# New queue orders for VectorE, ScalarE and GpSimd, and 54 waits of GpSimd for VectorE

## The chip, the cores and the metric

One Trainium2 chip; the kernel runs on one of its NeuronCores. The metric is the device time of one launch in microseconds. In the profile the engines are PE (TensorE, matmuls), PEld (its weight loads), DVE (VectorE), ACT (ScalarE), POOL (GpSimd) and SP (SyncE, which here issues the DMAs). L312 and the like are lines of the kernel before.

## The reference

A block with attention and a gated feed-forward part, both fed by the same normalised rows (sequence S = 2048, width D = 512, F = 1792, 32 heads of 16, a sliding window of 256), all float32:

```python
def _A_ref(x, wqkv, wo):                     # H = 32, Dh = 16, W = 256
    qkv = (x @ wqkv).reshape(B, S, 3, H, Dh).transpose(2, 0, 3, 1, 4)
    q, k, v = qkv[0], qkv[1], qkv[2]
    scores = jnp.einsum("bhqd,bhkd->bhqk", q, k) * (Dh ** -0.5)
    mask = (idx[:, None] - idx[None, :] >= 0) & (idx[:, None] - idx[None, :] < W)
    p = _softmax(jnp.where(mask[None, None], scores, -1e9), axis=-1)
    o = jnp.einsum("bhqk,bhkd->bhqd", p, v)
    return o.transpose(0, 2, 1, 3).reshape(B, S, D) @ wo

def _B_ref(x, w1, w3, w2):
    h = _silu(x @ w1) * (x @ w3)
    return h @ w2

xn = _layernorm(A_x, axis=-1)
return A_x + _A_ref(xn, A_wqkv, A_wo) * _silu(_B_ref(xn, B_w1, B_w3, B_w2))
```

## The kernel before, in words

**Arithmetic.** Every float32 operand of a large product is scaled and cut into two float16 parts, a high one and the rest (the low one), and a product is three matmul terms (high by high, low by high, high by low) that add up in a PSUM bank. So each weight tile of 128 by 512 costs, beside its load, a high part (ScalarE) and a subtraction for the low part, on VectorE or on GpSimd. `split` (L310 to L312) writes the high part on ScalarE (L311) and the low part in one VectorE operation (L312). `split_pool` (L319 to L323) scales the tile and copies the high part on ScalarE (L320, L321), and subtracts in four pieces on GpSimd (L323).

**Tiling.** The sequence is cut into four tiles of 512 rows. For each, the kernel projects q, k and v (L539, L572, L587 to L590), takes the maxima of the scores in a first pass (L637, L650), computes scores, their exponentials and the product with v in a second (L720 on TensorE, L726 the mask on VectorE, L728 the exponential on ScalarE, L746 on TensorE), and normalises the heads' outputs (L317 and L814 on GpSimd). Between these, in the same tile, stand the large products of the feed-forward part: gate and up (`gate_up`, L1004; its tanh on ScalarE is L1018, the two VectorE operations behind it are L1021 and L1025, its high part L1034 on ScalarE and its low part L317 on GpSimd), and down (L1224 in the first two tiles). In the last two tiles the down product is done by a scheme of seven products on combined halves (`fold_weights`, `fold_first`, `fold_second`; L1144), whose sums and cuts are GpSimd's work: L963 to L966 add the weight halves, L972 copies a high part on ScalarE, L975 copies one on GpSimd, L976 subtracts the low part. The sum of a row block with the attention's output is `total` (L1267 a tanh on ScalarE, L1268 on VectorE, L1273 on TensorE, L1276 and L1278 on VectorE); the last block is done in two halves by columns (`total_by_columns`, L1300 to L1310), each with a store of its own.

**Buffers.** 54 numbered slots of SBUF hold raw weights, cut parts and activations in turn; a program name such as slot53_832 is slot 53 with the number of the instruction that took it. Weights are squared and summed first (L230 and L894 on ScalarE) for a scale per tile, and only then cut.

**Order.** TensorE runs in the order in which the program is written. For VectorE, ScalarE, GpSimd and SyncE a table of numbers in `QUEUES` (L1608) gives the order: number k is the k-th instruction that the program makes for that engine, and `queue` chains each instruction to the one ahead of it, so that the engine issues them in that order. Semaphores between engines come from the data alone: a read after a write, or a buffer that is taken again. SyncE's table sets in which order the loads and stores are issued, each when its buffer's last user is done.

The place that the prediction dwells on is this pair in `total`:

```python
nc.scalar.activation(y, acc, AF.Tanh, scale=0.5)                                            # L1267
nc.vector.scalar_tensor_tensor(y, y, 1.0, acc, op0=ALU.add, op1=ALU.mult)                   # L1268
```

Of the kernel before, what the change touches and what calls it, by code (L numbers as in the profile page):

```python
# [17 lines left out]
ENGINE = mybir.EngineType  # L18
# [62 lines left out]
def tile_block(ctx: ExitStack, tc: tile.TileContext, x, wqkv, wo, w1, w3, w2, out):  # L81
# [1518 lines left out]
    for n, b in enumerate((1, 3, 0)):  # L1600
# [139 lines left out]
```

## Time and profile before

| | |
|---|---|
| median of 3 runs | 809.68 us (807.79 to 810.52) |
| the profiled execution | 809.6 us, of which the span of its instructions is 807.8 us |
| TensorE busy | 791.1 us (98%), 9181 matmuls |
| VectorE busy | 622.9 us (77%) |
| ScalarE busy | 394.8 us (49%) |
| GpSimd busy | 382.2 us (47%) |
| mean granted TensorE clock | 0.995 |

The profile is of one execution. A row of the timeline reads: start and length in us, engine, line and operation, what it writes and reads, how many instructions the row joins, and in brackets the idle time of the engine ahead of it and what ended that. Instructions of one engine overlap a little: the next one starts some 0.1 us before the one ahead ends, so the distance from start to start is what an instruction costs its queue. The view of waits lists for TensorE, per pair of line and releaser, the time waited in all, how often, and the longest. The view of windows gives busy time per engine and stretch, the granted clock, the share of time in which the DMA engines were busy, and GB/s.

### The profile page before, as it was taken

Reading aid. Unit: us, or ns where it says so; the run is one execution under the profiler, and the core shown is the slowest. Engines: PE = TensorE matmul, PEld = TensorE weight load, DVE = VectorE, ACT = ScalarE, POOL = GpSimd, SP = SyncE. Lnnn points to the kernel's source line nnn. Section 1 sums busy time; section 2 is a strip of 40 time slices with the busy share of each in tenths; the row PEclk is TensorE's granted clock in tenths of the full one; section 3 lists DMA queues with packets and bytes.
Section 4 is the critical chain, followed back from the end, with each engine's and each line's share of the span. In section 5 each row is a group of like instructions: output and inputs, shape, how many; then the busy total and the mean of one; then the engine's idle time right before and its main releaser. Section 6 shows DMA issues by size and latency. Waiting matters only on the chain.

```text
span 807.8 us, 23938 instructions
## 1 busy us (share of the span) xinstructions
PE 791.1 (98%) x9181; PEld 404.2 (50%) x9181; DVE 622.9 (77%) x2005; ACT 394.8 (49%) x592; POOL 382.2 (47%) x746
## 2 busy tenths in 40 slices
PE   8989999999997999999999999999999999999998
PEld 4434454444543444444444454456544654466465
DVE  8778989877897678777878887766677888775438
ACT  8779976734364355334534433444444344444411
POOL 2263857732428375265622356530246277550670
PEclk9999999999998999999999999999999999999999
DMA  9768674737563375757465634656462553335431
GB/s 282 220 187 270 218 228 128 250 111 225 161 209 128 103 260 139 237 159 261 132 218 165 185 94 142 165 152 184 121 182 75 161 145 110 111 88 160 127 94 58
DMA packets 109858, 134.18 MB, mean 166 GB/s; under 512 B 18928, under 2 KB 64944, under 8 KB 109744
## 3 DMA queue, kind: packets, MB, share of 16 engines
q1 hardware_dynamic: 109456, 132.13, 54.2%
q8 instruction: 72, 1.18, 0.6%
q10 hardware_dynamic: 288, 0.52, 0.2%
q14 instruction: 42, 0.34, 0.1%
HBM read 91.23 MB, written 36.57 MB: 158 GB/s over the span
## 4 chain that ended last, share of the span: by engine, by line
PE 74%; DVE 8%; DMA 7%; SPq 3%; POOL 3%; ACT 3%; issue 2%; DVEq 0%; ACTq 0%; POOLq 0%
PE m L1004 28%; PE m L1144 8%; PE po L746 8%; PE m L572 7%; PE m L1224 6%; PE s L720 5%; PE m L1273 5%; PE m L539 4%; PE s L637 2%; DMA slot<-in_B_w_dram 2%; DMA dWQ<-slot 2%; POOL slot L323 1%; PE po L637 1%; DVE s L726 1%; DVE junk L650 1%
## 5 line engine op out<-in xcount | busy, mean ns | idle before, releaser
L1004 PE MATMUL m<-XH,slot 128*128 128x512 f16 x896 | 269.0, 382 | 0.1
L728 ACT ACTIVATE pt<-s,es 128x1024 f32<-128x1024 f32 x152 | 167.0, 1113 | 145.2 <-DVE s L726 135.4
L1004 PEld LDWEIGHTS <-slot 128*128 128x128 f16 x1344 | 125.5, 98 | 155.7 <-issue 15.0
L1004 PE MATMUL m<-XL,slot 128*128 128x512 f16 x448 | 170.5, 381 | 0.0
L726 DVE TENSOR_TENSOR s<-s,MK 128x256 f32<-128x256 f32 (+2 forms) x280 | 120.3, 437 | 60.7 <-PE s L720 51.5
L650 DVE CUSTOM_DVE_ANT_0 junk<-s,MW 128x320 bf16<-128x320 f32 x276 | 121.7, 484 | 15.8 <-PE s L637 15.2
L317 POOL TENSOR_TENSOR slot<-slot,slot 128x256 f16<-128x256 f32 (+1 forms) x86 | 58.2, 695 | 90.2 <-ACT slot L1034 41.5
L323 POOL TENSOR_TENSOR slot<-slot,slot 128x128 f16<-128x128 f32 x168 | 66.6, 434 | 50.5 <-ACT slot L321 49.5
L1224 PE MATMUL m<-slot,slot 128*128 128x512 f16 x336 | 78.5, 380 | 0.1
L650 DVE CUSTOM_DVE_ANT_0 junk<-po,MW 128x320 bf16<-128x320 f32 x172 | 77.5, 484 | 0.0
L746 PE MATMUL po<-pt,V 64*32 64x320 f32 (+4 forms) x2880 | 77.2, 342 | 0.0
L572 PE MATMUL m<-XH,slot 128*128 128x512 f16 x240 | 70.8, 380 | 2.1 <-DVE slot L1021 2.1
L1018 ACT ACTIVATE slot<-m,sgs 128x512 f32<-128x512 f32 x56 | 38.3, 685 | 65.6 <-PE m L1004 63.6
L1144 PE MATMUL m<-slot,slot 128*128 128x256 f16 x588 | 68.3, 273 | 0.0
L1059 POOL TENSOR_TENSOR slot<-slot,slot 128x256 f16<-128x256 f32 x98 | 65.0, 672 | 1.5
L720 PE MATMUL s<-qa,KA 50*64 50x320 f16 (+3 forms) x1472 | 58.6, 261 | 6.3 <-ACT pt L728 6.3
L1021 DVE SCALAR_TENSOR_TENSOR slot<-slot,m 128x512 f32<-128x512 f32 x56 | 38.3, 684 | 31.1 <-ACT slot L1018 30.9
L1144 PEld LDWEIGHTS <-slot 128*128 128x128 f16 x588 | 56.2, 98 | 11.1 <-issue 2.7
L746 PEld LDWEIGHTS po<-pt,V 64*32 64x32 f32 x2880 | 50.3, 106 | 22.4 <-issue 0.8
L720 PEld LDWEIGHTS <-KA 50*64 50x64 f16 x1472 | 30.6, 106 | 58.0 <-issue 45.6
L572 PEld LDWEIGHTS <-slot 128*128 128x128 f16 x392 | 36.6, 98 | 44.1 <-issue 3.3
L317 POOL TENSOR_TENSOR on<-on,rb 128x256 f32<-128x256 f32 x32 | 23.3, 745 | 67.6 <-DMA rb<-de 64.4
(194 smaller groups left out, 1148.0 us busy)
## 6 DMA issues: line engine op xcount, KB each, us to landing
slot<-dW SPq DMA_DIRECT2D x98, 256.0 KB
slot<-in_B_w_dram SPq DMA_DIRECT2D x56, 256.0 KB
slot<-dFold SPq DMA_DIRECT2D x48, 256.0 KB
dW<-slot SPq DMA_DIRECT2D x42, 256.0 KB
slot<-in_A_x_dram SPq DMA_DIRECT2D x30, 256.0 KB
KA<-dK SPq DMA_DIRECT2D x24, 288.0 KB
slot<-dWQ SPq DMA_DIRECT2D x24, 256.0 KB
qa<-dQ SPq DMA_DIRECT2D x30, 192.0 KB
```

Source lines behind the costliest of these rows:

```text
L317: op(out[:, c], a[:, c], b[:, c])
L323: nc.gpsimd.tensor_sub(lo[:, c:c + P], raw[:, c:c + P], hi[:, c:c + P])
L572: nc.tensor.matmul(cell["pp"][:, cols[n]], w[:, (a * NC + c) * P:(a * NC + c + 1) * P], b[:, c, cols[n]], start=n == 0 and (c, i) == parts ...
L650: nc.vector.tensor_tensor_reduce(out=junk[:, :n], in0=s[:, r, :n], in1=mask, scale=1.0, scalar=NEG, op0=ALU.add, op1=ALU.max, accum_out=M[ ...
L720: nc.tensor.matmul(s[64 * h:64 * h + 64, r, o:o + 64 * n], ka[rows, 2 * p + a, 64 * (m + 4):64 * (m + 5)], qa[rows, 2 * p + a, 64 * (m + k ...
L726: nc.vector.tensor_add(v, v, MK[:, kind, of:of + n, :].unsqueeze(1).to_broadcast([P, 2 * len(which), n, 64]))
L728: nc.scalar.activation(pt, s, AF.Exp, scale=es)
L746: nc.tensor.matmul(cell["po"][32 * i:32 * i + 32, h, 64 * (m + k):64 * (m + k + n)], V[64 * h:64 * h + 64, (4 * t + m // 2) % VB, hd * VW: ...
L1004: nc.tensor.matmul(cell[k], w[:, (a * NC + c) * P:(a * NC + c + 1) * P], b[:, c, :], start=c == 0 and i == 0, stop=c == NC - 1 and i == 2)
L1059: nc.gpsimd.tensor_sub(lo, view, hi)
L1144: nc.tensor.matmul(cell["ps"][:, c], made[:, f:f + P], wj[:, g:g + 256], start=j == j0 and c == 0 and n == 0, stop=j == j1 - 1 and n == 2, ...
L1224: nc.tensor.matmul(ps, hh[:, a * TW + b * P:a * TW + (b + 1) * P], w[:, c * D:(c + 1) * D], start=f == f0 and i == 0, stop=f == f1 - 1 and ...
```

## The change

No instruction is added, taken out or given other operands. The order tables of VectorE, ScalarE and GpSimd are replaced; TensorE's and SyncE's orders stay as they are. Beside that, `give_way` adds 54 waits across engines, read from a list `TURNS`: in the pair 675-285, GpSimd's instruction 285 waits on a semaphore until VectorE's instruction 675 is done. Instruction numbers are the same as in `QUEUES`; the counting of them is moved into `numbered`. On VectorE's side of the pairs stand five L1268 (675, 705, 1328, 1366 and 1422), and small operations on maxima, scales, means and variances (L242, L277, L281, L283, L420, L424, L425, L452, L667, L668, L853, L854, L898, L918); on GpSimd's side mostly the subtractions and cuts L317, L323, L975, L976, L1058 and L1059.

```diff
 QUEUES = {
     ENGINE.DVE: (
...
-        "52-54 51 55-56 63 57 64 61 66 58 60 65 62 67 59 43 36 49 68 74-77 69 78-79 70 80-81 71 90 72-73 82-84 86-87 85 "
+        "52-54 51 55-56 63-64 57 61 66 60 58 65 62 67 43 36 49 59 68 74-77 69 78-79 70 80-81 71 90 72-73 82-84 86-87 85 "
...
     ENGINE.Activation: (
...
     ENGINE.Pool: (
...
+TURNS = (
+    "203-86 204-86 205-87 195-87 206-92 214-93 251-128 252-129 253-130 287-131 216-117 264-132 217-118 265-121 "
+    "259-134 311-162 312-135 313-140 314-149 315-150 343-171 344-159 362-154 350-204 366-190 431-191 423-210 "
+    "432-214 433-222 519-259 572-270 573-271 675-285 612-310 645-326 646-337 705-361 683-341 721-365 722-366 "
+    "758-392 759-402 795-397 796-399 924-460 1085-533 1223-587 1224-582 1328-622 1299-630 1300-633 1366-628 "
+    "1422-657 1374-676 "
+)
+
+
+def give_way(tc):
+
+
+    made = {e: numbered(tc, e) for e in (ENGINE.DVE, ENGINE.Pool)}
+    for pair in TURNS.split():
+        first, second = map(int, pair.split("-"))
+        tc.add_manual_dep(made[ENGINE.Pool][second], made[ENGINE.DVE][first].name,
+                          mybir.DependencyInfo(mybir.DependencyClass.Sync, mybir.DependencyReason.DATA), reason="turn")
+
+
+def numbered(tc, engine):
+
+
+    return [i for i in tc.nc.cur_bb.bb.instructions if i.engine == engine and i.opcode != "RegisterMove"
+            and not i.opcode.startswith("Tile")]
...
         for engine, order in QUEUES.items():
             queue(tc, engine, order)
+        give_way(tc)
```

**ScalarE's queue, about 45 us into the span** (the first gate products of the first tile). slot53_832 is the tanh of a gate product; the L894 and the L230 are squares of weights just loaded; slot1_907 and slot3_973 are high parts of projections. Before:

```order
L230 ACTIVATE sqa_824,ssq_805<-slot36_699 128x512
L1034 CAST slot46_788<-slot45_734 128x512
L230 ACTIVATE sqa_841,ssq_805<-slot38_703 128x512
L1018 ACTIVATE slot53_832<-m0_809,sgs_155 128x512
L320 ACTIVATE slot18_209<-slot18_209,pi_756 128x512
L894 ACTIVATE sqa_843,ssq2_736<-slot42_711 128x512
L321 CAST slot52_817<-slot18_209 128x512
L230 ACTIVATE sqa_882,ssq_805<-slot37_700 128x512
L587 ACTIVATE slot1_907<-m1_885 128x512
L230 ACTIVATE sqa_899,ssq_805<-slot39_704 128x512
L320 ACTIVATE slot19_210<-slot19_210,pi_756 128x512
L321 CAST slot5_834<-slot19_210 128x512
```

Now:

```order
L1018 ACTIVATE slot53_832<-m0_809,sgs_155 128x512
L230 ACTIVATE sqa_824,ssq_805<-slot36_699 128x512
L320 ACTIVATE slot18_209<-slot18_209,pi_756 128x512
L230 ACTIVATE sqa_841,ssq_805<-slot38_703 128x512
L321 CAST slot52_817<-slot18_209 128x512
L587 ACTIVATE slot1_907<-m1_885 128x512
L894 ACTIVATE sqa_843,ssq2_736<-slot42_711 128x512
L320 ACTIVATE slot19_210<-slot19_210,pi_756 128x512
L230 ACTIVATE sqa_882,ssq_805<-slot37_700 128x512
L321 CAST slot5_834<-slot19_210 128x512
L230 ACTIVATE sqa_899,ssq_805<-slot39_704 128x512
L587 ACTIVATE slot3_973<-m0_912 128x512
```

The tanh L1018 of slot53_832 stood behind two L230 and the L1034 of slot46_788, and stands now ahead of them, directly behind two L894. That L1034 has gone 15 places back, out of this piece. The L587 of slot3_973 ends the piece now; before it stood two places below the piece, behind one more L320 (that of slot20, which now follows it).

**GpSimd's queue, about 239 to 251 us into the span** (the sums and cuts of the folded down weights). The L323 are low parts of weights cut on ScalarE; L975 and L976 cut a folded weight; the two L976 of slot48_4683 are the last readers of slot27_3790, and the L1267 of slot27_5415 on ScalarE, which takes that buffer over, waits for them. Before:

```order
L975 CAST slot24_4642<-slot31_4360 128x256 x2
L976 TENSOR_TENSOR slot24_4642<-slot31_4360,slot24_4642 128x256
L323 TENSOR_TENSOR slot28_4260<-slot51_3582,slot28_4260 128x128 x4
L323 TENSOR_TENSOR slot42_4259<-slot46_3581,slot42_4259 128x128 x4
L323 TENSOR_TENSOR slot30_4262<-slot47_3584,slot30_4262 128x128 x4
L323 TENSOR_TENSOR slot29_4261<-slot14_3583,slot29_4261 128x128
L317 TENSOR_TENSOR slot2_4338<-slot21_4249,slot2_4338 128x256 x2
L323 TENSOR_TENSOR slot29_4261<-slot14_3583,slot29_4261 128x128 x3
L976 TENSOR_TENSOR slot48_4683<-slot27_3790,slot48_4683 128x256 x2
L963 TENSOR_TENSOR slot5_4518<-slot33_4174 128x256
L965 TENSOR_TENSOR slot34_4519<-slot35_4175,slot33_4174 128x256
L964 TENSOR_TENSOR slot5_4518<-slot35_4175,slot5_4518 128x256
```

Now:

```order
L976 TENSOR_TENSOR slot22_4586<-slot45_4361,slot22_4586 128x256
L323 TENSOR_TENSOR slot28_4260<-slot51_3582,slot28_4260 128x128 x4
L323 TENSOR_TENSOR slot42_4259<-slot46_3581,slot42_4259 128x128 x4
L323 TENSOR_TENSOR slot30_4262<-slot47_3584,slot30_4262 128x128 x4
L323 TENSOR_TENSOR slot29_4261<-slot14_3583,slot29_4261 128x128 x2
L317 TENSOR_TENSOR slot2_4338<-slot21_4249,slot2_4338 128x256 x2
L323 TENSOR_TENSOR slot29_4261<-slot14_3583,slot29_4261 128x128 x2
L976 TENSOR_TENSOR slot48_4683<-slot27_3790,slot48_4683 128x256 x2
L963 TENSOR_TENSOR slot5_4518<-slot33_4174 128x256
L965 TENSOR_TENSOR slot34_4519<-slot35_4175,slot33_4174 128x256
L964 TENSOR_TENSOR slot5_4518<-slot35_4175,slot5_4518 128x256
L317 TENSOR_TENSOR slot15_4484<-slot23_4422,slot15_4484 128x256 x2
```

One L976 of slot22_4586 and the two L975 and one L976 of slot24_4642 no longer stand ahead of the L323; they come behind the last row shown. The L317 of slot15_4484, instruction 285, has come forward past one L975 and one L966, and its first half now waits for instruction 675 of VectorE, the L1268 of slot27_5415.

**VectorE's queue at the end of the program** (the last row blocks of the last tile). slot5_13731 is the last block, done in two halves by columns (L1309, L1310). Before:

```order
L1278 TENSOR_TENSOR slot31_13673<-slot31_13673,slot4_13439 128x512
L1278 TENSOR_TENSOR slot19_13694<-slot19_13694,slot38_13441 128x512
L1276 SCALAR_TENSOR_TENSOR slot24_13713<-m0_13712,us_4326,slot24_13713 128x512
L1301 SCALAR_TENSOR_TENSOR slot5_13731<-slot5_13731,slot46_13654 128x512
L1278 TENSOR_TENSOR slot24_13713<-slot24_13713,slot47_13670 128x512
L1309 SCALAR_TENSOR_TENSOR slot5_13731<-m1_13734,us_4326,slot5_13731 128x256
L1310 TENSOR_TENSOR slot5_13731<-slot5_13731,slot43_13691 128x256
L1309 SCALAR_TENSOR_TENSOR slot5_13731<-m0_13750,us_4326,slot5_13731 128x256
L1310 TENSOR_TENSOR slot5_13731<-slot5_13731,slot43_13691 128x256
```

Now:

```order
L1278 TENSOR_TENSOR slot31_13673<-slot31_13673,slot4_13439 128x512
L1276 SCALAR_TENSOR_TENSOR slot24_13713<-m0_13712,us_4326,slot24_13713 128x512
L1301 SCALAR_TENSOR_TENSOR slot5_13731<-slot5_13731,slot46_13654 128x512
L1309 SCALAR_TENSOR_TENSOR slot5_13731<-m1_13734,us_4326,slot5_13731 128x256
L1278 TENSOR_TENSOR slot19_13694<-slot19_13694,slot38_13441 128x512
L1278 TENSOR_TENSOR slot24_13713<-slot24_13713,slot47_13670 128x512
L1309 SCALAR_TENSOR_TENSOR slot5_13731<-m0_13750,us_4326,slot5_13731 128x256
L1310 TENSOR_TENSOR slot5_13731<-slot5_13731,slot43_13691 128x256 x2
```

The first L1309 has moved ahead of the L1278 of slot19 and slot24, and both L1310 stand behind the second L1309.

More of the change, by code (lines that the diff above doesn't have):

```diff
@@ L1702 @@
 }
+TURNS = (
[5 rows of a table added]
+)
[8 more added lines that the diff above has]
+            and not i.opcode.startswith("Tile")]
 def queue(tc, engine, order):
-    made = [i for i in tc.nc.cur_bb.bb.instructions if i.engine == engine and i.opcode != "RegisterMove" and not i.opcode.startswith("Tile")]
+    made = numbered(tc, engine)
     spans = [tuple(map(int, s.split("-"))) for s in order.split()]
     line = [made[k] for s in spans for k in range(s[0], s[-1] + 1)]
-    assert len(line) == len(made), (engine, len(made), len(line), [(i.name, i.opcode) for i in made[:12]], [(i.name, i.opcode) for i in made[-5:]])
+    assert len(line) == len(made)
     for before, after in zip(line, line[1:]):
```

127 rows, old and new, of the table QUEUES are left out of this document.

## The prediction

> **What bounds the kernel now.** First the page's table of busy times:
>
> ```profile
> PE 791.1 (98%) x9181; PEld 404.2 (50%) x9181; DVE 622.9 (77%) x2005; ACT 394.8 (49%) x592; POOL 382.2 (47%) x746
> ```
>
> TensorE is busy for 791.1 of 807.8 us. No instruction goes or comes, so no busy time changes except where a queue was blocked: what an order can win is TensorE's idle time and lost clock. Next, its waits (in all, times, longest):
>
> ```profile
> PE s L720 <- ACT pt L728: 6.3, 3, 5.3
> PE m L572 <- DVE slot L1021: 2.1, 1, 2.1
> PE s L539 <- DVE p2qk L283: 0.7, 1, 0.7
> PE s L637 <- DMA qa<-dQ: 0.2, 1, 0.2
> ```
>
> Third, where they lie, by windows (PE, PEld, DVE, ACT, POOL busy, granted clock, DMA share, GB/s):
>
> ```profile
> 44.00:56.00 12.00, 9.95 (x76) 4.32 (x74) 7.15 (x36) 10.78 (x25) 5.64 (x14) 1.00 0.30 92
> 250.00:256.00 6.00, 1.85 (x9) 0.75 (x8) 5.97 (x4) 2.13 (x4) 4.57 (x8) 1.00 0.12 44
> 256.00:264.00 8.00, 6.68 (x42) 2.86 (x42) 5.85 (x21) 4.33 (x5) 5.13 (x9) 0.57 0.40 131
> 264.00:780.00 516.00, 515.95 (x6438) 266.26 (x6437) 384.21 (x1181) 214.91 (x277) 243.83 (x416) 1.00 0.52 152
> ```
>
> From 264 to 780 us TensorE has no gap: the new orders can win nothing there and can only lose. All that is to be had lies ahead of 264 us, most of it at one place, which also halves the clock (0.57 in the window behind it).
>
> **The stall at 251.9 us.** The timeline there, TensorE first, then ScalarE, VectorE and GpSimd:
>
> ```profile
> 249.09 0.61 PE L1004 MATMUL m<-XH,slot 128*128 128x512 f16 x2
> 251.04 0.59 PE L1004 MATMUL m<-XH,slot 128*128 128x512 f16 x2
> 251.47 0.38 PE L1004 MATMUL m<-XL,slot 128*128 128x512 f16 x1
> 257.18 1.32 PE L720 MATMUL s<-qa,KA 50*64 50x320 f16 x24 [5.33 <-ACT pt L728]
> 258.87 1.01 PE L1004 MATMUL m<-XH,slot 128*128 128x512 f16 x2
> 262.67 0.89 PE L1004 MATMUL m<-XH,slot 128*128 128x512 f16 x2
> ```
>
> ```profile
> 249.28 0.63 ACT L1267 ACTIVATE slot<-slot 128x512 f32<-128x512 f32 x1 [0.86 <-POOL slot L976]
> 256.02 1.11 ACT L728 ACTIVATE pt<-s,es 128x1024 f32<-128x1024 f32 x1 [3.88 <-DVE s L726]
> ```
>
> ```profile
> 249.94 5.17 DVE L1268 SCALAR_TENSOR_TENSOR slot<-slot,slot 128x512 f32<-128x512 f32 x1 [2.56 <-ACT slot L1267]
> 255.03 0.89 DVE L726 TENSOR_TENSOR s<-s,MK 128x256 f32<-128x256 f32 x2
> ```
>
> ```profile
> 237.23 0.74 POOL L975 CAST slot<-slot 128x256 f16<-128x256 f32 x2 [8.05 <-DMA dW<-slot]
> 237.93 1.30 POOL L976 TENSOR_TENSOR slot<-slot,slot 128x256 f16<-128x256 f32 x2
> 240.51 5.06 POOL L323 TENSOR_TENSOR slot<-slot,slot 128x128 f16<-128x128 f32 x13
> 247.94 1.30 POOL L976 TENSOR_TENSOR slot<-slot,slot 128x256 f16<-128x256 f32 x2
> 250.58 0.74 POOL L964 TENSOR_TENSOR slot<-slot,slot 128x256 f32<-128x256 f32 x1
> 252.29 1.30 POOL L317 TENSOR_TENSOR slot<-slot,slot 128x256 f16<-128x256 f32 x2
> 253.89 0.68 POOL L976 TENSOR_TENSOR slot<-slot,slot 128x256 f16<-128x256 f32 x1
> ```
>
> The L1268 lasts 5.17 us, though at the end of the program, with GpSimd quiet, a like one takes 0.69 (the L1278 quoted under the tail, same shape, two SBUF inputs). It ends at 255.11; GpSimd ran without a break from 237.23 to 254.57. So it was let in only when GpSimd stopped, and then took its 0.5 to 0.7. Behind it stand in VectorE's queue the mask L726, then ScalarE's L728, then TensorE's L720.
>
> Two edits meet here. First, one L976, two L975 and one L976 move from ahead of the L323 to behind: 238.58 to 240.51, that is 1.95 us from start to start with the L976's 0.65. The two L976 that release L1267 then end at 249.24 − 1.95 = 247.29, L1267 runs to 247.96, and L1268 is issued at 248.0. Second, GpSimd's L317 (252.29) now waits for it. Ahead of that wait still stand the L964 and its two neighbours, which end at 251.32 − 1.95 = 249.37. Then GpSimd is quiet, and L1268 ends at 249.37 + 0.54 = 249.9, against 255.11: **5.2 us** for L726, L728 and L720. L728 would end at 257.13 − 5.2 = 251.93, TensorE has work to 251.85: the stall closes to a tenth. Queued behind the waiting L317 are its second half, L966, two L975 and further L976, some 0.6 us late against their new place and earlier than in the old one; the moved cuts of slot22 and slot24 come behind those, near where the old run ended, and no row of TensorE waits for a L976. Bounds: 5.33 if the port were free at once; 3.1 if the 1.95 us are not gained but the wait works (L1268 ends at 251.32 + 0.65 = 252.0).
>
> **The clock.** Nine matmuls L1004 took 1.95 us from 249.09 to 251.04 and, after the stall, 3.80 from 258.87 to 262.67: 1.85 us lost, and a little in the 28 matmuls from 257.18; I take **2.1**. The other long idle time, 2.06 us at 49.83, left the clock at 1.00 (first window). So an idle time between 2.06 and 5.33 us is where the loss starts, and a closed stall has none. The Trainium skill, "TensorE: Matmul & The Clock Gate", Part 1, says that the clock halves after an idle window of about 3.4 us and comes back after as much work; the trace agrees at both places. Estimated by it, a rest of stall under 3.4 us would keep the full clock.
>
> **The stall at 47.8 us.**
>
> ```profile
> 46.63 0.63 ACT L230 ACTIVATE sqa<-slot 128x512 bf16<-128x512 f32 x1
> 47.26 0.60 ACT L1034 CAST slot<-slot 128x512 f16<-128x512 f32 x1
> 48.39 0.67 ACT L1018 ACTIVATE slot<-m,sgs 128x512 f32<-128x512 f32 x1
> 49.09 0.69 DVE L1021 SCALAR_TENSOR_TENSOR slot<-slot,m 128x512 f32<-128x512 f32 x1 [3.41 <-ACT slot L1018]
> 49.83 0.59 PE L572 MATMUL m<-XH,slot 128*128 128x512 f16 x2 [2.06 <-DVE slot L1021]
> 54.30 0.57 ACT L587 ACTIVATE slot<-m 128x512 f16<-128x512 f32 x1
> ```
>
> L1018 takes the place of the L230 at 46.63, so L1021 and L572 come 48.39 − 46.63 = 1.76 us earlier (ScalarE shows no idle time ahead of L1018, so its product was ready; how long, no row says). But ScalarE is busy for 10.78 of 12 us here: what is queued behind L1018, the two L230, the cuts and the L587 of 54.30, comes as late as the work ahead of it takes. Of the work ahead of that L587 only the L1034 and one L320 have gone behind it: 0.60 and, like it, 0.6 to 0.7, less 0.1 of overlap each, so it starts near 53.1, 1.2 earlier. Its bank is what the next gate product needs: TensorE gets back about **1.15** of the 1.76, and waits some 0.6 there. Bounds 0.5 (the L1034 alone) and 1.76.
>
> **The two smaller L720.**
>
> ```profile
> 92.97 0.42 PE L720 MATMUL s<-qa,KA 50*64 50x320 f16 x10 [0.45 <-ACT pt L728]
> 159.52 0.42 PE L720 MATMUL s<-qa,KA 50*64 50x320 f16 x10 [0.52 <-ACT pt L728]
> ```
>
> ScalarE's new order puts cuts (L320, L321) behind these L728, and VectorE's puts small operations on scales behind the masks ahead of them, each some 0.6 us, more than either wait: both go, **0.97**; at worst nothing. The waits of L539 and L637 at the start I leave as they are: some small operations pass ahead of VectorE's L312 there, and behind them TensorE waits for the load qa all the same, which covers some tenths; without that cover they would cost about 0.5.
>
> **The tail.**
>
> ```profile
> 802.49 0.69 DVE L1278 TENSOR_TENSOR slot<-slot,slot 128x512 f32<-128x512 f32 x1
> 803.10 0.48 DVE L1309 SCALAR_TENSOR_TENSOR slot<-m,us,slot 128x256 f32<-128x256 f32 x1
> 803.95 0.48 DVE L1309 SCALAR_TENSOR_TENSOR slot<-m,us,slot 128x256 f32<-128x256 f32 x1
> 804.46 0.42 DVE L1310 TENSOR_TENSOR slot<-slot,slot 128x256 f32<-128x256 f32 x1
> ```
>
> The first L1309 now starts where a L1278 did, at 802.49; two L1278 at 0.61 from start to start, the second L1309 and two L1310 follow: 802.49 + 0.51 + 1.22 + 0.51 + 0.34 + 0.42 = 805.5 instead of 804.88, so 0.6 later. The last two stores then leave 0.3 us apart instead of 0.8: **+0.7**, between 0 and 0.9.
>
> **Sum**, against the profiled execution's 809.6 us (1.8 outside the span; the median shown, 809.68, is the same): 809.6 − 5.2 − 2.1 − 1.15 − 0.97 + 0.7 = 800.9, so **801 us**. All bounds at their best give 809.6 − 5.33 − 2.1 − 1.76 − 0.97 = 799.4, and with the 0.9 us of waits at the start 798.5.
>
> **Rivals.** *The stall shrinks, but does not close* (0.17). GpSimd's run begins when a store of folded weights lands (237.23, idle 8.05 before): if that does not move up with the 2 us that TensorE gains earlier, or the 1.95 us are lost, L1268 ends at 252.0, TensorE idles 2.2, and the time is 803; with both, idle 4.3 and the clock lost again, 807. For it: that wait for DMA. Against: that store's data come from the same chain, which moves with TensorE.
>
> *The gain is given back by the next lock* (0.08). Only 54 pairs are named; another L1268 or L726 that meets a run of GpSimd costs again 5.2 + 2.1: 808.2. For it: the orders are all new. Against: over 516 us from 264 TensorE showed no wait in spite of 243.83 us of GpSimd work.
>
> *Slower: the turns hold GpSimd's cuts back* (0.07). 29 of the 54 turns lie between 83 and 160 us, where L1224 reads weights that GpSimd's L323 has just cut, and several of them now stand behind VectorE operations that themselves wait for TensorE. The tightest I find:
>
> ```profile
> 129.24 1.11 ACT L728 ACTIVATE pt<-s,es 128x1024 f32<-128x1024 f32 x1 [0.91 <-DVE s L726]
> 132.44 2.33 PE L1224 MATMUL m<-slot,slot 128*128 128x512 f16 x10
> ```
>
> The L321 that a cut of four L323 needs now stands behind this L728: 130.35, plus 0.6, plus four at 0.39 (5.06 / 13), so 132.5; L1224 reads it some four matmuls into its ten, near 133.3. That leaves under 1 us, and one turn more or less. If each of the 29 cost TensorE 0.4 us, 11.6 would be added to 800.9: 812.5; slower than before from 0.3 each (8.7 / 29). Against: no L323 is among TensorE's waits, and GpSimd is 47% busy.
>
> *The port is let go between two GpSimd instructions* (0.04). Then L1268, issued at 248.0, would end near 249.3 whatever the wait: 800.4. The 5.17 us speak against it, with GpSimd instructions starting at 250.58, 252.29 and 253.89 inside it. The Trainium skill, "SBUF — State Buffer", section "SBUF: two separate sides", states it so: the lock is held for the whole instruction, and the loser waits; here the trace has it wait for a whole run.
>
> **Numbers.** The forecast, with its own range of 799 to 803, has 0.64. The 8-in-10 range is 798 to 806: from all bounds at their best to most of the first rival. About 0.3%, 2.4 us, can be told from no change. Faster: 0.64 + 0.04 + 0.14 + 0.03 of the second = 0.85; same: 0.03 + 0.05 = 0.08; slower: 0.07.
>
> **What would show it.** L1268 near 248 us should last about 2 us instead of 5.17 and L317 on GpSimd start behind it; TensorE's wait for L728 should fall from 6.3 to under 1; the clock should stay at 1.00 in all windows; the wait of L572 for L1021 should be 0.3 or less, with one of about 0.6 a little later. I am wrong if a wait for GpSimd's L323 stands in TensorE's list, or a gap shows after 264 us.

## The result

| | before | changed |
|---|---|---|
| median | 808.80 us (807.79 to 810.52, 4 runs) | 798.58 us (798.28 to 798.97, 4 runs) |
| the profiled execution | 809.6 us, span 807.8 | 798.36 us, span 796.5 |
| mean granted clock | 0.995 | 0.999 |

The ratio is 0.9872, with a 95% interval of 0.9851 to 0.9892: 10.2 us faster, where 801 us were forecast and a range of 798 to 806. The page's busy times after:

```profile
PE 788.6 (99%) x9181; PEld 403.3 (51%) x9181; DVE 616.6 (77%) x2005; ACT 396.1 (50%) x592; POOL 381.3 (48%) x746
```

TensorE's busy time is 2.5 us less with the same 9181 matmuls (the stretch at half clock is gone), VectorE's 6.3 less with the same 2005 instructions. Most of that is time held: the operations that last over 0.2 us longer than the shortest of their line and size are too long by 15.3 us together in the old trace, and by 9.6 in the new one. TensorE's waits after, and its windows:

```profile
PE s L539 <- DVE wvl L312: 1.4, 2, 1.0
PE m L1495 <- DVE onesb L183: 1.0, 1, 1.0
PE m L468 <- DVE slot L452: 0.5, 1, 0.5
PE s L265 <- DVE sb L242: 0.2, 1, 0.2
```

```profile
44.00:56.00 12.00, 12.00 (x95) 5.17 (x93) 8.59 (x41) 11.21 (x26) 4.96 (x14) 1.00 0.47 146
250.00:256.00 6.00, 6.00 (x129) 3.06 (x127) 5.03 (x18) 2.74 (x3) 6.00 (x13) 1.00 0.65 201
256.00:770.00 514.00, 514.00 (x6342) 266.04 (x6340) 381.23 (x1173) 215.41 (x278) 245.24 (x419) 1.00 0.53 153
```

The waits for L728 (6.3 us in all before) and L1021 (2.1) are out of the list; what is left stands in the first 27 us. The window of the big stall, 1.85 of 6 us busy before, is full, and the clock stays at 1.00.

The timeline of the place of the big stall, VectorE, GpSimd, ScalarE, then TensorE:

```profile
243.97 1.52 DVE L1268 SCALAR_TENSOR_TENSOR slot<-slot,slot 128x512 f32<-128x512 f32 x1
245.42 0.89 DVE L726 TENSOR_TENSOR s<-s,MK 128x256 f32<-128x256 f32 x2
```

```profile
232.81 0.74 POOL L975 CAST slot<-slot 128x256 f16<-128x256 f32 x2 [6.97 <-DMA dW<-slot]
234.15 5.45 POOL L323 TENSOR_TENSOR slot<-slot,slot 128x128 f16<-128x128 f32 x14
244.23 0.72 POOL L964 TENSOR_TENSOR slot<-slot,slot 128x256 f32<-128x256 f32 x1
245.64 1.31 POOL L317 TENSOR_TENSOR slot<-slot,slot 128x256 f16<-128x256 f32 x2 [0.69 <-ACT slot L587]
```

```profile
246.40 1.11 ACT L728 ACTIVATE pt<-s,es 128x1024 f32<-128x1024 f32 x1 [0.19 <-DVE s L726]
```

```profile
248.44 0.64 PE L720 MATMUL s<-qa,KA 50*64 50x320 f16 x24
```

GpSimd stops after L964 at 244.95. L1268 ends at 245.49, the same 0.54 us behind that as in the old trace, and L317 starts 0.15 behind L1268. The releaser named for L317 is an instruction of ScalarE that ended at 245.60; that VectorE's instruction is the one that held GpSimd off is shown by the runs without that wait, below. L728 ends at 247.51, and L720 follows the matmul ahead of it without a gap.

### The profile page after: what moved, and what is told of

Same layout as the page of the kernel before. It is cut to its first block, busy times and chain, and to the rows that moved or that the text cites. A ratio compares the mean times of both kernels' runs of the same rounds, so it can differ in the third digit from the quotient of the medians.

```text
span 796.5 us, 23974 instructions
## 1 busy us (share of the span) xinstructions
PE 788.6 (99%) x9181; PEld 403.3 (51%) x9181; DVE 616.6 (77%) x2005; ACT 396.1 (50%) x592; POOL 381.3 (48%) x746
## 3 DMA queue, kind: packets, MB, share of 16 engines
q8 instruction: 72, 1.18, 0.7%
## 4 chain that ended last, share of the span: by engine, by line
PE 94%; DVE 3%; DMA 2%; ACT 1%; issue 0%; SPq 0%; DVEq 0%
PE m L1004 38%; PE po L746 9%; PE m L572 9%; PE m L1224 9%; PE m L1144 8%; PE s L720 6%; PE m L1273 5%; PE m L539 5%; PE s L637 3%; PE po L637 2%; DMA slot<-in_A_wqkv_dram 1%; DMA slot<-in_A_x_dram 0%; PE s L488 0%; DMA slot<-in_B_w_dram 0%; DVE junk L232 0%
## 5 line engine op out<-in xcount | busy, mean ns | idle before, releaser
L1004 PE MATMUL m<-XH,slot 128*128 128x512 f16 x896 | 267.3, 380 | 0.0
L728 ACT ACTIVATE pt<-s,es 128x1024 f32<-128x1024 f32 x152 | 167.2, 1114 | 142.7 <-DVE s L726 133.8
L1004 PEld LDWEIGHTS <-slot 128*128 128x128 f16 x1344 | 124.9, 98 | 154.1 <-issue 11.7
L1004 PE MATMUL m<-XL,slot 128*128 128x512 f16 x448 | 169.8, 379 | 0.0
L726 DVE TENSOR_TENSOR s<-s,MK 128x256 f32<-128x256 f32 (+2 forms) x280 | 120.5, 438 | 59.8 <-PE s L720 50.0
L317 POOL TENSOR_TENSOR slot<-slot,slot 128x256 f16<-128x256 f32 (+1 forms) x86 | 58.7, 699 | 75.1 <-ACT slot L1034 30.4
L323 POOL TENSOR_TENSOR slot<-slot,slot 128x128 f16<-128x128 f32 x168 | 66.7, 433 | 45.9 <-ACT slot L321 45.3
L1224 PE MATMUL m<-slot,slot 128*128 128x512 f16 x336 | 78.5, 380 | 0.0
L1018 ACT ACTIVATE slot<-m,sgs 128x512 f32<-128x512 f32 x56 | 38.4, 686 | 69.2 <-PE m L1004 69.0
L572 PE MATMUL m<-XH,slot 128*128 128x512 f16 x240 | 70.8, 380 | 0.0
L1059 POOL TENSOR_TENSOR slot<-slot,slot 128x256 f16<-128x256 f32 x98 | 65.1, 672 | 1.8
L720 PE MATMUL s<-qa,KA 50*64 50x320 f16 (+3 forms) x1472 | 58.0, 259 | 0.0
L1021 DVE SCALAR_TENSOR_TENSOR slot<-slot,m 128x512 f32<-128x512 f32 x56 | 38.3, 683 | 25.2 <-ACT slot L1018 24.9
L572 PEld LDWEIGHTS <-slot 128*128 128x128 f16 x392 | 36.5, 98 | 42.0 <-issue 1.0
L720 PEld LDWEIGHTS <-KA 50*64 50x64 f16 x1472 | 30.0, 105 | 51.5 <-issue 40.0
L1025 DVE SCALAR_TENSOR_TENSOR slot<-m,slot 128x512 f32<-128x512 f32 x56 | 38.6, 689 | 18.7 <-PE m L1004 18.1
```

The lines of the kernel that those rows point to most:

```text
L317: op(out[:, c], a[:, c], b[:, c])
L323: nc.gpsimd.tensor_sub(lo[:, c:c + P], raw[:, c:c + P], hi[:, c:c + P])
L572: nc.tensor.matmul(cell["pp"][:, cols[n]], w[:, (a * NC + c) * P:(a * NC + c + 1) * P], b[:, c, cols[n]], start=n == 0 and (c, i) == parts ...
L720: nc.tensor.matmul(s[64 * h:64 * h + 64, r, o:o + 64 * n], ka[rows, 2 * p + a, 64 * (m + 4):64 * (m + 5)], qa[rows, 2 * p + a, 64 * (m + k ...
L726: nc.vector.tensor_add(v, v, MK[:, kind, of:of + n, :].unsqueeze(1).to_broadcast([P, 2 * len(which), n, 64]))
L728: nc.scalar.activation(pt, s, AF.Exp, scale=es)
```

## The experiments

All times are medians, with the lowest and highest. The runs were made in three series, each on one chip with runs of the kernel before beside them; half a microsecond is compared only within a series. In the runs without some of the waits, the lowest and highest matter more than the median, since what they leave out turns out to happen in some executions and not in others.

### All waits out, orders kept

```diff
-TURNS = ("203-86 204-86 205-87 ... 1374-676 ")
+TURNS = ""
```

> The changed kernel with all 54 waits left out, orders kept. Theory (VectorE's operation on two SBUF inputs is let in only when GpSimd's run of instructions ends, and one of the 54 waits makes that end): GpSimd goes on from L964 without a break through L317, L966, L975 and one L976 to about 248.2 us and stops only because its next L976 needs ScalarE's L972, queued behind the L728 that the L1268 holds up; L1268, issued at 244.0, ends near 248.8 instead of 245.5, 3.3 us later; 0.9 us of that is slack, so TensorE idles some 2.3 us at L720, without loss of clock: about 800.9 us. Rival one (the port is let go between two GpSimd instructions): L1268 lasts 1 to 1.5 us as with the waits, 798.6 us. Rival two (many of the 54 matter): several new waits of TensorE, 803 us or more.

Measured: 803.97 us (800.31 to 809.79, 7 runs), ratio to before 0.9929 (0.9896 to 0.9962). The profiled execution is the slowest one, 809.79:

```profile
L1268 DVE SCALAR_TENSOR_TENSOR slot<-slot,slot x15: 677/685/5081, 250.4 to 798.7; 128x512 f32<-128x512 f32 x15
```

```profile
153.85 4.77 DVE L854 TENSOR_TENSOR p<-pp 128x2 f32<-128x2 f32 x1
158.61 0.68 DVE L590 SCALAR_TENSOR_TENSOR slot<-m,slot 128x512 f16<-128x512 f32 x1
```

```profile
159.34 0.62 PE L572 MATMUL m<-XH,slot 128*128 128x512 f16 x2 [3.00 <-DVE slot L590]
257.57 0.42 PE L720 MATMUL s<-qa,KA 50*64 50x320 f16 x12 [2.61 <-ACT pt L728]
```

The long L1268 is back, 5.08 us, and so is a wait at L720, 2.61 us, near the 2.3 expected. Beside it an operation on 128 by 2 numbers, 0.15 us at its shortest, lasts 4.77 us, and TensorE loses 3.0 us there. The clock halves after both waits, which was not expected of waits that short. So the first theory holds for the place, and is too small for the whole. The time, 803.97, is the one that rival two gave, and new waits are there as it said; how much hangs on the one wait and how much on the others, the runs below tell.

### The one wait, in the old orders

```diff
-TURNS = ("203-86 ... 675-285 ... 1374-676 ")
+TURNS = "675-285"
```

with the three order tables of before.

> The kernel before, orders untouched, with the one wait 675-285 added. Theory: GpSimd stops in front of L317 when L966 ends at 252.3 us, L1268 ends 0.5 us later at 252.9 instead of 255.1, and TensorE's idle time falls from 5.3 to 3.1 us: 2.2 us won, 806.6 us, if the clock is still lost, and 804.5 us if an idle time of 3.1 us leaves it at full. Rival (per instruction): L1268 was not held by the run, nothing changes, 808.8 us.

Measured: 807.08 us (805.1 to 809.9, 10 runs), ratio 0.9972 (0.9953 to 0.9990): 0.8 to 3.8 us won. In the profiled execution (806.75) the three engines read:

```profile
249.18 2.94 DVE L1268 SCALAR_TENSOR_TENSOR slot<-slot,slot 128x512 f32<-128x512 f32 x1 [1.99 <-ACT slot L1267]
```

```profile
250.84 0.73 POOL L966 TENSOR_TENSOR slot<-slot,slot 128x256 f32<-128x256 f32 x1
252.27 1.29 POOL L317 TENSOR_TENSOR slot<-slot,slot 128x256 f16<-128x256 f32 x2 [0.69 <-DVE slot L1268]
```

GpSimd stops at 251.57, L1268 ends 0.55 us later, L317 waits for it. The theory's mechanism stands, and so does its size (L1268 lasts 2.94 us instead of 5.17); the longest wait of L720 is 2.5 us, and the clock still falls (0.57 from 256 to 260 us), so the variant "3.1 us leaves it at full" is out.

### The piece of GpSimd's order, with and without the wait

Both runs keep before's orders but for 58 places of GpSimd's:

```diff
     ENGINE.Pool: (
...
-274 255 257-258 256 259-262 276 291-292 294 293 295-296 298 297 267-270 263-266 281-284 277 271-272 278-280
-304-305 287 289 288 313 290 285-286 315 314 317-318 316 306 299 307 309 308 310 302-303
+257-258 255-256 259-262 274 276 291-292 294 293 267-270 263-266 281-284 277-278 271-272 279-280 304-305 287
+289 288 285-286 290 313 315 314 317-318 316 295 306 296 298 297 299 307 302-303 309 308 310
...
```

The first has `TURNS = "675-285"`, the second `TURNS = ""`.

> The kernel before with only the piece of GpSimd's order from 230 to 262 us as in the change, and the one wait 675-285. Theory: the stall and the clock's loss go as in the change, 8.3 us by its trace (7.3 in the prediction): 800.5 to 801.5 us, L1268 about 2 us long. Rival (the rest of the change, which moves GpSimd's work up against TensorE, is needed too): TensorE still idles 1 to 2 us, 802 to 803 us.

> The same piece of GpSimd's order in the kernel before, without any wait. Theory: L1268 is issued at 248.0 us, GpSimd's run goes on to about 252.6, so it ends near 253.2 instead of 255.1: 1.9 us won, 806.9 us with the clock lost, 804.8 with it kept. Then neither part does much alone and both do it together. Rival (the order does it, the wait nothing): 800.5 to 801.5 us.

Measured: with the wait 803.06 us (801.10 to 810.32, 7 runs), ratio 0.9941 (0.9900 to 0.9983); without it 804.10 us (801.01 to 809.32, 10 runs), ratio 0.9943 (0.9913 to 0.9973). The two can't be told apart. For the first, the median lies above the 800.5 to 801.5 expected and only the fastest executions come near; at 250 us, though, its trace has no stall (L1268 lasts 1.79 us). For the second, the theory was wrong at 250 us and the rival right: there the order does it without the wait. Its trace:

```profile
247.98 1.40 DVE L1268 SCALAR_TENSOR_TENSOR slot<-slot,slot 128x512 f32<-128x512 f32 x1
259.77 6.59 DVE L667 TENSOR_SCALAR NM<-M 128x16 f16<-128x16 f32 x1
```

```profile
251.43 1.30 POOL L317 TENSOR_TENSOR slot<-slot,slot 128x256 f16<-128x256 f32 x2 [2.60 <-ACT slot L1034]
```

```profile
269.26 2.72 PE L1224 MATMUL m<-slot,slot 128*128 128x512 f16 x6 [4.27 <-DVE slot L1021]
```

L1268 takes 1.40 us, without any wait added: GpSimd stops by itself behind L964, for 2.60 us, because L317 needs ScalarE's L1034, which in the old ScalarE order stands behind two L961. In the first run GpSimd stops there for L1034 too (1.91 us), so the added wait did nothing in its trace. In the new ScalarE order L1034 stands ahead of the two L961, which takes this pause away; there the added wait puts it back (next runs). Both traces show what the prediction listed as the next lock: L667, 0.16 us at its shortest, lasts 6.59 us in the second (TensorE waits 4.27 us and the matmuls behind it go at half clock) and 3.10 us in the first (TensorE waits 1.14 us). The pair 612-310 of the changed kernel is a wait for this L667; there it lasts 1.25 us and TensorE waits for nothing.

### The one wait in the new orders, and its complement

The change again as the measure, then its orders with the one wait, with the 53 others, and with none:

```diff
-TURNS = ("203-86 ... 675-285 ... 1374-676 ")
+TURNS = "675-285"
```

> The changed kernel once more, as the measure for the runs beside it on the same chip: 798 to 799 us, and within 1 us from run to run, if its waits keep every VectorE operation out of GpSimd's long runs.

> The changed kernel's orders with only the wait 675-285, the other 53 left out. Theory one (the prediction's: only the L1268 of the big stall matters, elsewhere TensorE had no such wait): 798 to 799.5 us. Theory two (from the run without any wait: in these orders L277 near 139 us and L854 near 154 us are caught in GpSimd's long runs of L323 for 3.1 and 4.8 us, which costs TensorE 0.9 and some 5 us with the lost clock): median 801 to 804 us, a spread of several us, a full clock at 250 us.

> The changed kernel with 53 of the waits, the one in front of the L1268 of the big stall (675-285) left out. Theory (this one wait carries the place at 250 us, where the run without waits lost 5.0 us: 2.7 of idle time and the rest by a clock at half): 803.5 to 804.5 us, with a spread of about 1 us, since the other waits keep the earlier places out of chance. Rival (the orders alone part L1268 from GpSimd's run in most executions): 799 to 800 us in most runs and a few of 804.

> The changed orders with the wait 675-285 alone, on the same chip as its complement. Theory one (the other 53 do nothing that can be measured): 799.3 to 800 us in every run. Theory two (they take out a chance event: L854 near 154 us caught by a run of L323 in some executions, some 5 us each time, as in the profile of the run without any): most runs at 799.7, one in four or so at 803 to 806 us.

> The changed orders without any wait, beside its two halves. If the one wait and the 53 act apart from each other, the loss here is the sum of theirs: 5 us for the one, 0 to 5 for the others by chance: median 804 to 805, from 800 to 810 as before. If the spread there came from the chip or the hour, now 804 to 805 within 1 us.

| waits | series | median | single executions |
|---|---|---|---|
| all 54 | second | 799.35 us | 798.90, 799.15, 799.55, 799.64 |
| 675-285 alone | second | 799.65 us | 799.35, 799.65, 799.66, 799.71 |
| 675-285 alone | third | 800.30 us | 799.41, 799.87, 800.30, 805.19, 805.80 |
| the other 53 | third | 803.96 us | 798.61, 803.83, 803.96, 804.59, 804.83 |
| none | third | 805.16 us | 804.43, 804.76, 805.57, 806.68 |

The kernel before: 809.74 us (805.80 to 813.12, 7 runs) in the second series, 810.46 us (806.31 to 810.74, 9 runs) in the third.

The changed kernel itself came out at 799.35 us in the second series, just above the 798 to 799 expected. Taking out the one wait costs 4.6 us (803.96 against 799.35, in different series; in the third series the change with only VectorE's old tail, the last run below, stands at 798.01), in four executions of five. In the fifth, 798.61, nothing is lost, so the orders alone part the two engines only sometimes, and the spread is 6 us where about 1 was expected. The trace of the slowest of the five, 804.83:

```profile
245.12 5.17 DVE L1268 SCALAR_TENSOR_TENSOR slot<-slot,slot 128x512 f32<-128x512 f32 x1 [0.70 <-ACT slot L1267]
```

```profile
245.76 0.72 POOL L964 TENSOR_TENSOR slot<-slot,slot 128x256 f32<-128x256 f32 x1
246.46 1.29 POOL L317 TENSOR_TENSOR slot<-slot,slot 128x256 f16<-128x256 f32 x2
249.08 0.66 POOL L976 TENSOR_TENSOR slot<-slot,slot 128x256 f16<-128x256 f32 x1
```

```profile
252.36 0.42 PE L720 MATMUL s<-qa,KA 50*64 50x320 f16 x12 [3.47 <-ACT pt L728]
```

L317 follows L964 at once, GpSimd runs on to 249.74, L1268 ends 0.55 us later, TensorE idles 3.47 us, and the granted clock is at half from 254.1 to 257.5 us. This is the prediction's mechanism, with the one wait as the only difference from the changed kernel.

Without any wait the L1268 lasts 5.18 us in the third series' trace and all four executions lose 5.1 to 7.3 us against 799.35: about what the one wait is worth, and up to 3 us more, as expected if the two parts act apart. The spread there is 2.3 us, where the first series had 9.5; why it differs is not shown.

With the one wait alone, seven of the nine executions are within a microsecond or so of the change, and two lose some 5 us. The median of the second series, 799.65, lies just above the range of theory one and far under the 801 to 804 of theory two. There is one small thing that the other 53 do in every trace. L277 near 139 us, 0.16 us at its shortest, is held in all four traces of the new orders without the 53; here in that of 799.35 us:

```profile
138.43 3.17 DVE L277 TENSOR_SCALAR al<-al 128x4 int32<-128x4 int32 x1
```

```profile
144.62 0.59 PE L1004 MATMUL m<-XH,slot 128*128 128x512 f16 x2 [0.72 <-DVE slot L1246]
```

In the traces with the 53 it lasts 0.20 us at most, and TensorE has no wait for L1246. The medians differ by 0.3 us (799.65 against 799.35), with ranges that overlap. The profiled execution of the third series, 805.19, is one of the two that lose more:

```profile
239.11 6.43 DVE L668 SCALAR_TENSOR_TENSOR NM<-M,NM 128x16 f16<-128x16 f32 x1
```

```profile
245.93 0.48 PE L637 MATMUL s<-KA,qa 48*64 48x320 f16 x4 [4.17 <-DVE XL L497]
```

A third operation, at a third place, and again held until GpSimd's run ends. So a chance event of some 5 us is there, as theory two of the third series said, but not at the operation it named. With all 54, the four executions of the second series and the four of the result lie between 798.28 and 799.64 us; the twelve of the three runs below have all 54 as well and lie between 797.56 and 800.32. None of these twenty loses 5 us, where two of nine did.

### ScalarE's piece undone

```diff
     ENGINE.Activation: (
...
-47-48 45 43 49-50 55 54 52 58 53 64 59 56 60 57 63 67 61-62 65-66 51 70 68-69
+48 47 45 43 49-50 54 51 58 55 52 59 53 60 64 63 56-57 61 67 62 65-66 68-70
...
```

> The changed kernel with the piece of ScalarE's order from 42 to 57 us as before (L1018 of slot53 again behind two L230 and the L1034). Theory: TensorE waits about 2 us for L1021 at 48 us again and nothing else changes: 2.1 us more, 800.7 us. Rival (the prediction's bound: only 1.15 us are won there, or the lateness is taken up elsewhere): 0.5 to 1.2 us more.

Measured: 800.22 us (799.82 to 800.32, 4 runs), beside 799.35 (798.90 to 799.64) for the change in the same series: 0.87 us more. TensorE waits 1.61 us at L572 again:

```profile
49.48 0.59 PE L572 MATMUL m<-XH,slot 128*128 128x512 f16 x2 [1.61 <-DVE slot L1021]
```

but the waits of L1004 for L590 that the change's trace of that series has behind it (0.5 us in two) are not there. So the rival, the bound that the prediction had worked out from ScalarE's queue, is right: of the 1.61 us, 0.87 show in the time, and the rest is given back at the next bank.

### VectorE's start and tail undone

```diff
     ENGINE.DVE: (
...
-1452 1455-1456 1451 1453 1457-1459 1461 1454 1460 1469 1462 1465 1463 1470 1472 1467 1466 1464 1473 1475
-1468 1471 1476 1478-1479 1474 1477 1481 1480 1482
+1451-1452 1455 1457 1456 1453 1459 1461 1458 1465 1454 1469 1460 1462-1463 1467 1470 1472 1475 1466 1473
+1464 1468 1471 1474 1476 1478 1477 1479-1482
```

The first run has the first 70 places as before too.

> The changed kernel with VectorE's order as before in its first 70 places and from place 1451 to the end. Theory: the 0.6 to 0.7 us lost in the tail come back, and of the 1.4 us of waits of L539 for L312 at the start some 0.3: 797.6 us, 0.9 under the changed kernel; the last L1310 ends some 1.1 us behind TensorE's last matmul as before, instead of 1.6. Rival (the load qa ends the wait at the start and the last stores' landing sets the end in any order): 0.3 us or less.

> The changed kernel with VectorE's order as before from place 1451 on, and nothing else. Theory (the run with old start and tail: its gain of 0.7 us at the start was used up at the load qa by 30 us, its tail ended 0.7 us earlier): 0.5 to 0.7 us under the changed kernel, 798.6 to 798.9 us. Rival: within 0.3 us of it.

Measured: with both, 798.84 us (798.47 to 799.59, 4 runs), 0.5 under the change in the same series, between the 0.9 of the theory and the 0.3 of the rival, with ranges that overlap. With the tail alone, 798.01 us (797.56 to 798.30, 4 runs), ratio to before 0.9853 (0.9838 to 0.9868), below what was expected, but in a series without the change beside it. The traces say more about the tail. The last matmul group and VectorE's last operation, first of the change, then of the run with the old tail:

```profile
789.02 2.78 PE L1307 MATMUL m<-slot,slot 128*128 128x256 f16 x24
```

```profile
792.67 0.75 DVE L1310 TENSOR_TENSOR slot<-slot,slot 128x256 f32<-128x256 f32 x2
```

```profile
789.22 2.95 PE L1307 MATMUL m<-slot,slot 128*128 128x256 f16 x24
```

```profile
793.12 0.42 DVE L1310 TENSOR_TENSOR slot<-slot,slot 128x256 f32<-128x256 f32 x1
```

VectorE ends 1.62 us behind TensorE in the change (791.80, 793.42), 1.37 with the old tail (792.17, 793.54); the span ends 4.7 and 4.3 us behind it (796.5 and 796.4). Over all traces, the span ends 4.67 to 4.69 us behind the last matmul in the eight with the new tail and 3.96 to 4.27 in the six with the old one. So the old tail is worth 0.4 to 0.7 us. The kernel with it has the lowest median of all that ran; that it is the fastest is not shown by the times, which come from different series, but only by this difference in the traces.

## Why the prediction was right, and where its sizes were off

The n-th matmul of one trace can be set against the n-th of the other. The steps in the distance between them, by the rows quoted here and there:

```profile
47.83 0.59 PE L572 MATMUL m<-XH,slot 128*128 128x512 f16 x2
```

```profile
90.34 0.42 PE L720 MATMUL s<-qa,KA 50*64 50x320 f16 x10
156.30 0.42 PE L720 MATMUL s<-qa,KA 50*64 50x320 f16 x10
```

| step of the prediction | predicted | between the two traces |
|---|---|---|
| the stall behind L1268 | −5.2 | −5.4 (distance 3.34 ahead of it, 8.74 at L720) |
| the clock behind it | −2.1 | −2.9 (8.74 at L720, 11.68 once the clock is full again) |
| the stall at 47.8 us | −1.15 | −2.1 (2.26 at L572, 0.15 lost at the next bank); undone alone, 0.87 |
| the two smaller L720 | −0.97 | −1.1 (0.51 and 0.59) |
| the start | 0 | +0.26 by 30.3 us |
| the tail | +0.7 | +0.7 (last matmul 12.0 us earlier, span 11.3 shorter) |
| not in the sum | | −0.7 (0.26 at L1224 near 80 us, 0.12 near 230, 0.30 near 389) |
| sum | −8.7 | −11.2 |

**The stall.** The chain was read rightly: L1268 held by GpSimd, then L726, L728, L720; the wait in front of L317 ends the run, and L1268 ends 0.54 us behind it. Taking out that wait alone brings a L1268 of 5.17 us back, in the trace shown; one execution of the five went without. Two details of the step were off. L1268 was put at 248.0 with about 2 us; in the time of the old trace it was issued at 247.3 and took 1.52, since the run of GpSimd ahead of it moved up by 4.42 us (237.23 to 232.81) where TensorE had moved up by 3.34. And the step left out what ScalarE's order does: in the old one L317 would have had to wait for L1034 anyway, once it came forward, so that the moved piece of GpSimd's order was enough there (1.40 us without any wait). The wait is needed because L1034 comes earlier in the new order.

**The clock.** The mechanism held and its term was mis-sized: the 28 matmuls from 257.18, which the step counted as "a little", lose 0.88 us between them, and 2.06 go to the L1004 up to 263.1. What the step took for a safe rest of stall, under 3.4 us, is refuted: 2.4 us were enough for the loss (last section).

**The stall at 47.8 us.** In the profiled pair the term was nearly double. Part of that is not the order: the two L894 ahead of L1018, which wait for a load, start 0.4 us earlier in the new trace (44.70, against 45.12), and with them the whole queue. L587 starts at 52.47 instead of 54.30, 1.83 earlier, not 1.2. The run that undoes this piece alone puts its worth at 0.87 us, inside the bounds of 0.5 and 1.76.

**The tail and the small waits** came as worked out in size. The small waits have no run of their own, and neither have most of the changed places: some 840 places of the three tables hold another instruction than before, and for those outside the runs above only the matched matmuls speak.

**The rivals.** The next lock, given 0.08, is real: L854, L667 and L668 are each held for 4.6 to 6.4 us in one of the runs. It doesn't strike in the changed kernel, in eight executions. Pairs of the list stand at these very operations (366-190 for that L854, 612-310 for L667, 573-271 for L668); the prediction had not credited the 53 with that. That each of these pairs by itself keeps its operation free was not run. That GpSimd's cuts are held back to TensorE's cost, the slower case, did not happen: no L323 is in the list of waits. The tight place near 133 us showed no wait either. The price of the rival with the port let go, 800.4, does not fit the prediction's own bound: of 5.33 us of idle time only 0.13 are left behind the 5.2, so it should have read 800.8.

The median gain, 10.2 us, is less than the 11.2 of the profiled pair; before's executions differ among themselves by several us (803.29 to 812.72 in 25 runs of the first series), which the prediction did not foresee, having three. It was worked out from one execution of before. That this one, at 809.6, lies near the median of 808.80 was luck: in the fastest of the 25 the granted clock is 1.000, so the clock's loss, at least, is not in every execution. The time itself, 798.58, lies 0.6 us inside the lower end of the range and below the 799 to 803 of the forecast's own.

## What to carry to other kernels

When an operation of a fraction of a microsecond shows up with several, look at what GpSimd did in the same window (or VectorE, if the operation is GpSimd's) before looking at its inputs. A semaphore wait that stopped GpSimd in front of its next instruction cost it 0.69 us here and let VectorE in; put it where VectorE's operation is on the way to TensorE. And time such a kernel several times: a spread of some us, from one execution to the next, can be a sign of such a collision. Here, in the second series, it fell from 7.3 us (seven executions of the old kernel) to 0.7 (four of the changed one), so a fix can show in the spread as well as in the median.

## What the runs showed of the hardware

**Held for one instruction, or for a run of them.** Of the old trace's VectorE operations, 25 last over 0.2 us longer than the shortest of their line and size. In 23 the excess is at most 0.71 us, about the rest of one GpSimd instruction, although GpSimd goes on in most of them. One such pair:

```profile
309.78 1.25 DVE L1268 SCALAR_TENSOR_TENSOR slot<-slot,slot 128x512 f32<-128x512 f32 x1
```

```profile
309.75 0.73 POOL L317 TENSOR_TENSOR slot<-slot,slot 128x256 f32<-128x256 f32 x1 [0.98 <-DVE slot L1276]
310.44 1.87 POOL L317 TENSOR_TENSOR on<-on,rb 128x256 f32<-128x256 f32 x2
```

Here the same L1268 is let in when the first L317 ends (310.48; it ends 0.55 later), and GpSimd's next one pays, 1.18 us instead of 0.73. So the prediction's "let in only when GpSimd stopped" is wrong as a rule: it is right for two operations of that trace (held 4.50 and 2.16 us), and for those held 3.0 to 6.4 us in the runs above, through up to 13 GpSimd instructions. One stands between: the L667 of 3.10 us in the run with the piece and the wait was held over seven GpSimd instructions, and let in while GpSimd went on without a break. The Trainium skill, "SBUF — State Buffer", section "SBUF: two separate sides", has the pair held for one whole instruction; the 23 agree with it, the others do not. What decides between the two could not be settled: both occur with the same operation and the same line on GpSimd, and at one place in some executions and not in others. Operations with one SBUF input are held as well (L667, L277), while L1025, which reads one input from PSUM, takes at most 0.69 us beside GpSimd's runs.

**The clock falls after less than the idle time assumed.** Idle times of TensorE and the granted clock behind them: 1.61 us (the run with ScalarE's piece undone) and 2.06 us (before, ahead of 49.83), no loss; 2.4 us, half clock, in the run with the piece of GpSimd's order alone:

```profile
PE m L572 <- DVE slot L1021: 2.4, 1, 2.4
```

```profile
48.00:50.00 2.00, 0.04 (x1) 0.04 (x1) 0.78 (x2) 2.00 (x5) 1.29 (x2) 1.00 0.02 6
50.00:53.00 3.00, 3.00 (x22) 1.03 (x25) 1.78 (x9) 3.00 (x9) 1.59 (x4) 0.50 0.00 1
```

The same goes for 2.5, 2.6, 3.0 and 3.47 us in the other runs. By the clock's records the stretch at half lasts 3.41 us behind each of these and behind the 4.17 us of the run with the one wait alone, and 6.83 us behind the 4.27 us of the run shown and the 5.33 us of the old trace. It need not begin where TensorE goes on: behind the 3.47 us, which end at 252.36, it begins at 254.1. The Trainium skill, "TensorE: Matmul & The Clock Gate", Part 1, names an idle window of about 3.4 us; in these runs, with one or two such places in each, the loss starts between 2.06 and 2.4 us of idle time, and the measurement decides. Whether the length of the idle time alone sets it was not tested.
